# Query feature sums moved behind four half projections, and burst places of other double steps rewritten, in a gated mix of two linear-attention branches

## The chip, the cores and the metric

The kernel runs on one core of one Trainium2 chip. The metric is the device time of one execution in microseconds, as the median of the runs shown.

## The reference

One input x (2048 tokens, 640 features, 32 heads of 20) goes through two attention branches, A and B, and a gate mixes them:

```python
g = sigmoid((x * gate_w).sum(-1, keepdims=True))
a = A(x, wqkv, w_phi, wo)       # softmax features of q and k, linear attention over all tokens
b = B(x, wq, wk, wv, wo, beta)  # 4 segments of 512 tokens, local softmax plus a memory
return g * a + (1 - g) * b
```

Branch B is what the change touches. Its core, for each segment s:

```python
phi = lambda t: where(t > 0, t + 1, exp(t))
a_dot = softmax(qs @ ks.T * scale + causal_mask) @ vs
a_mem = (phi(qs) @ M) / (phi(qs) @ z + 1e-6)
o = sigmoid(beta) * a_mem + (1 - sigmoid(beta)) * a_dot
M, z = M + phi(ks).T @ vs, z + phi(ks).sum(tokens)
```

All inputs are bf16.

## The kernel before

Branch A comes first. It ends with a loop (L638 to L681) in which POOL adds the two halves of each token chunk (oA, L666) and SP turns the result (L674); meanwhile ACT evicts the first projections of branch B (L596), and SP turns them (L602). The query features of chunk 4, the first chunk of segment 1, have their exponential there too (L659), so that only their sum is left.

Branch B runs as 16 *double steps* (L966 to L996). A step is one group of four heads of one segment, a double step is two of them, a and b; four double steps make a segment. Each double step has five *bursts* of logits: PE multiplies keys by queries (L736, PSUM tile st_ps), and ACT takes the exponential of two tiles of 128x1024 (L740, into PT). POOL clears the triangles above the diagonal (L747). There are two st_ps tiles, so PE may run one tile ahead of ACT and then waits.

Between the bursts PE does other work, the *items*. A string of letters per double step (PLAN, L950) lists them in order, and a list of four shares per double step (SHARES, L955) says how far down the list PE gets after each of the first four bursts. After the fifth it does the rest. Every item has a weight, the estimated PE time in us; an item goes in after burst n as long as the weight done so far plus half its own is below share n of the whole (L992). The letters:

- h: half a projection of one chunk of 128 tokens for q, k or v of the next segment: five matmuls (L922), then an eviction of 128x320 by DVE (L928). With the second half of a q or k chunk, SP turns the chunk (L602).
- f and o: half an output row block, five or ten matmuls (L866), and its eviction by DVE (L875 or L877). A second half of f also stores the row (L879, on SP).
- A and D, B and C: the products of PT and values (L790), memory products (L798, L803) and the epilogue on DVE and POOL (L815 to L837), of step a of this double step (A, D) and of step b of the last one (B, C). Products go to one PSUM tile, nda.
- k and q, weight 0: the exponential of a chunk's features (L894, ACT).
- x and y, weight 0: the sum of a chunk's features for k and q, two DVE instructions (L897 takes the minimum with 1, L898 adds the positive part).
- z, weight 0: the transpose of the query features into the place of the consumed input (L907, on SP). It pairs with an earlier y.
- t, weight 0: the transpose of a finished chunk of branch B (L841, SP). u, weight 0: the four transposes of the last segment (L960, SP), which the closing part reads (L1046).

The matmuls of h, f and o write to one pool of two PSUM banks (tag ps1, L852). The third half in a row needs the bank of the first, and so the eviction of it.

The order on PE, ACT, DVE, POOL and SP is the order of the program (manual schedule): an instruction that waits holds all behind it on its engine. In double step 0 the halves h are the two halves of chunk 5 of k and the two of q, and the first y is the sum for chunk 4 of q.

Of the kernel before, what the change touches and what calls it, by code (L numbers as in the profile page):

```python
# [15 lines left out]
def kernel(  # L16
# [670 lines left out]
    with ExitStack() as bctx:  # L687
# [247 lines left out]
        def half_items(s, order):  # L935
# [11 lines left out]

        PLAN = ("qyhhhhozkxooAD", "qhhBhyChkzoxAooD", "qhhBhyChkzoxAooD",  # L950
                "ooBqoyoCokzoxADo", "hkhBhhChhqyhADztt", "khhBhxhqChfhyzAD",
                "khhBhxhqChfyzADt", "khhBhxhqChfyhzAD", "khhxtBhhqChyhADzt",
                "hhBhhqChfyhzAD", "hhBhhqCfhyzAthD", "hhBhhqhCftyhzAtD",
                "fBfCffADt", "fBftCfftAD", "fBftCffADf", "fuBfCfAfDf")
        SHARES = [[0.2, 0.42, 0.55, 0.77], [0.19, 0.4, 0.6, 0.85], [0.21, 0.4, 0.6, 0.8], [0.19, 0.4, 0.6, 0.81], [0.19, 0.41, 0.58, 0.8], [0.19, 0.41, 0.63, 0.86], [0.2, 0.4, 0.6, 0.83], [0.2, 0.4, 0.6, 0.83], [0.2, 0.4, 0.6, 0.8], [0.23, 0.4, 0.6, 0.82], [0.2, 0.4, 0.6, 0.82], [0.21, 0.4, 0.6, 0.82], [0.2, 0.4, 0.59, 0.8], [0.2, 0.39, 0.6, 0.8], [0.19, 0.4, 0.59, 0.8], [0.2, 0.4, 0.6, 0.85]]  # L955

        oT4 = oTA[:, 0:4]

# [7 lines left out]
        for dstep in range(NSEG * G // 2):  # L966
# [4 lines left out]
            items = []  # L971
            for w in PLAN[dstep]:
                if w in "hfo":
# [16 lines left out]
            for n, burst in enumerate(bursts(a, b)):  # L990
                burst()
                while items and (n == 4 or done + items[0][0] / 2 < SHARES[dstep][n] * whole):  # L992
                    w, fn = items.pop(0)
# [149 lines left out]
```

## Time and profile before

| what | us |
|---|---|
| median of three runs | 320.29 |
| the three runs | 320.96, 318.81, 320.29 |
| the profiled execution | 319.04 |
| its span on the core | 317.3 |
| PE busy / ACT busy / DVE busy / POOL busy | 303.7 / 252.8 / 225.4 / 209.2 |
| branch B's double steps, first exponential to the end of the last | 127.97 to 306.53 |

The span is the time from the first to the last recorded instruction of the profiled execution. Times of the trace count from the span's start. Busy times of PE overlap in a pipeline, so a busy PE need not be at its peak; a wait is what shows it held. The granted PE clock is 1.00 in every double step.

### The profile page before, as it was taken

What the parts mean: (1) busy time and instruction counts of PE and PEld (TensorE: products, weight loads), DVE (VectorE), ACT (ScalarE), POOL (GpSimd) and SP (SyncE); (2) the same over time, 40 slices, a digit from 0 to 9 for tenths busy, and PEclk for the clock granted to TensorE, in tenths of its full rate; (3) what the DMA queues carried; (4) which work ended last, traced back from release to release, by engine and by line L of the source; (5) the groups of instructions that cost most, each with busy time, mean ns of one, the idle gap of its engine ahead of it and who ended that gap; (6) DMA issues with size and microseconds to landing.
All of it is one profiled execution on the core that took longest, in us unless ns stands there. A gap on an engine that the chain in (4) does not pass through costs nothing.

```text
span 317.3 us, 9775 instructions
## 1 busy us (share of the span) xinstructions
PE 303.7 (96%) x4024; PEld 209.2 (66%) x4024; DVE 225.4 (71%) x505; ACT 252.8 (80%) x321; POOL 209.2 (66%) x308
## 2 busy tenths in 40 slices
PE   7999999999999999789999999999999999999995
PEld 7788877855578888356655566665656666656673
DVE  3477897998779997857668587778655864454463
ACT  5677888367846648799999899999989898898953
POOL 8588599103247989855656667778787777756550
PEclk9999999999999999999999999999999999999999
DMA  7949844439127989744331353473654443222132
GB/s 215 223 111 203 200 110 128 129 99 366 56 19 136 127 122 150 138 79 70 69 68 33 68 108 70 89 109 61 102 98 89 87 90 66 75 71 58 48 89 83
DMA packets 91814, 34.22 MB, mean 108 GB/s; under 512 B 79866, under 2 KB 91770, under 8 KB 91770
## 3 DMA queue, kind: packets, MB, share of 16 engines
q1 hardware_dynamic: 91194, 32.95, 49.3%
q10 hardware_dynamic: 576, 0.66, 0.8%
q8 instruction: 31, 0.51, 0.7%
q14 instruction: 13, 0.11, 0.1%
HBM read 6.42 MB, written 2.62 MB: 29 GB/s over the span
## 4 chain that ended last, share of the span: by engine, by line
PE 69%; ACT 21%; DVE 2%; issue 2%; DMA 2%; POOL 2%; SPq 1%; ACTq 0%; DVEq 0%; POOLq 0%
ACT PT L740 19%; PE st_ps L736 9%; PE proj L922 9%; PE proj L866 9%; PE pk L235 7%; PE pq L402 7%; PE pv L235 7%; PE nda L790 6%; PE proj L538 5%; PE num L460 3%; DMA x_nat<-in_A_x_dram 2%; PE kv_ps L375 2%; PE num L477 1%; DVE tt L508 1%; POOL oA L666 1%
## 5 line engine op out<-in xcount | busy, mean ns | idle before, releaser
L740 ACT ACTIVATE PT<-st_ps 128x1024 bf16<-128x1024 f32 x160 | 153.5, 1023 | 14.7 <-PE st_ps L736 12.7
L747 POOL TENSOR_SCALAR_AFFINE_SELECT PT<-PT 128x512 bf16<-128x512 bf16 (+1 forms) x130 | 87.0, 688 | 48.7 <-ACT PT L740 48.6
L790 PEld LDWEIGHTS <-PT 128*128 128x128 bf16 x1280 | 40.4, 96 | 9.6 <-issue 5.8
L790 PE MATMUL nda<-vB,PT 128*128 128x21 bf16 x1240 | 41.9, 173 | 0.1
L247 POOL TENSOR_TENSOR EkSn<-Ek,krec 128x1280 bf16<-128x1280 bf16 x15 | 35.1, 2360 | 8.8 <-DVE krec L246 8.1
L922 PEld LDWEIGHTS <-xTf 128*128 128x128 bf16 x300 | 26.4, 97 | 16.1 <-issue 7.7
L928 DVE CAST Z<-proj 128x320 bf16<-128x320 f32 x44 | 21.0, 488 | 21.3 <-PE proj L922 21.3
L235 PEld LDWEIGHTS <-xTf 128*128 128x128 bf16 x240 | 27.1, 113 | 5.8
L409 ACT ACTIVATE Eq<-pq 128x1024 bf16<-128x1024 f32 x20 | 19.4, 1021 | 12.3 <-PE pq L402 12.3
L243 DVE TENSOR_REDUCE ksum<-Ek 128x64 f32<-128x1280 bf16 x16 | 23.6, 1475 | 7.6 <-ACT Ek L239 7.4
L866 PE MATMUL proj<-WkA,oTA 128*128 128x320 bf16 x160 | 28.2, 300 | 0.0
L508 DVE TENSOR_TENSOR tt<-num,rr 128x640 f32<-128x640 f32 x32 | 25.0, 813 | 4.5 <-POOL rr L501 1.7
L239 ACT ACTIVATE Ek<-pk 128x640 bf16<-128x640 f32 x32 | 20.8, 702 | 9.2 <-PE pk L235 8.2
L666 POOL TENSOR_TENSOR oA<-tt 128x640 bf16<-128x640 f32 x16 | 24.7, 1550 | 5.2 <-DVE tt L508 5.0
L736 PE MATMUL st_ps<-Z 32*128 32x384 bf16 (+3 forms) x256 | 24.0, 299 | 3.9 <-ACT PT L740 3.3
L736 PE MATMUL st_ps<-Eq 32*128 32x512 bf16 (+3 forms) x256 | 24.7, 299 | 2.4 <-ACT PT L740 1.9
L402 PE MATMUL pq<-xTf,WqA 128*128 128x512 bf16 x100 | 22.2, 379 | 0.0
L830 POOL TENSOR_TENSOR oB<-td 128x320 bf16<-128x320 f32 x22 | 19.0, 863 | 4.1 <-DVE td L827 4.1
L866 PE MATMUL proj<-WvA,oT 128*128 128x320 bf16 x120 | 21.3, 300 | 0.0
L827 DVE TENSOR_TENSOR td<-nda,rec 128x640 f32<-128x640 f32 x23 | 19.0, 825 | 2.1
L922 PE MATMUL proj<-WqB,xTf 128*128 128x320 bf16 x110 | 17.8, 300 | 1.8 <-DVE Z L928 1.8
L538 PEld LDWEIGHTS <-xTf 128*128 128x128 bf16 x180 | 16.2, 97 | 4.6
(177 smaller groups left out, 548.6 us busy)
## 6 DMA issues: line engine op xcount, KB each, us to landing
Z<-EkSn SPq DMA_DIRECT2D x32, 160.0 KB, 2.8
out_dram<-orow SPq DMA_DIRECT2D x8, 160.0 KB, 1.8
out_dram<-oTA SPq DMA_DIRECT2D x6, 160.0 KB, 1.9
WvA<-in_A_wqkv_dram SPq DMA_DIRECT2D x2, 400.0 KB, 6.7
WvB<-in_B_wv_dram SPq DMA_DIRECT2D x1, 800.0 KB
WkB<-in_B_wk_dram SPq DMA_DIRECT2D x1, 800.0 KB, 6.7
WqB<-in_B_wq_dram SPq DMA_DIRECT2D x1, 800.0 KB, 8.4
WkA<-in_A_wo_dram SPq DMA_DIRECT2D x1, 800.0 KB, 10.1
```

The lines of the kernel that those rows point to most:

```text
L235: nc.tensor.matmul(ps[:, bk, 0:n], lhsT=key_tokens(c, sc), rhs=rhs, start=(c == 0), stop=(c == KC - 1))
L247: (nc.vector if sc == NCH - 1 else nc.gpsimd).tensor_tensor(out=EkSn[:, sc].rearrange("p s (h f) -> p (s h) f", f=DH), in0=Ek.rearrange("p ...
L402: nc.tensor.matmul(pq[:, half, :], lhsT=WqA[:, c, j * P:(j + 1) * P], rhs=xq[:, 2 * qb + half, c], start=(c == 0), stop=(c == KC - 1))
L508: nc.vector.tensor_tensor(out=tt[:, sgn].rearrange("p (b h) d -> p b h d", b=2), in0=ps, in1=csb, op=ALU.mult)
L538: nc.tensor.matmul(ps, lhsT=xq[:, sc // 4, cc, sc % 4 * P:(sc % 4 + 1) * P], rhs=W[:, cc, half * 320:(half + 1) * 320], start=(cc == 0), s ...
L666: nc.gpsimd.tensor_tensor(out=oA.rearrange("p (h d) -> p h d", d=DH), in0=tt[:, 0], in1=tt[:, 1], op=ALU.add)
L736: nc.tensor.matmul(ps[:, i - i0, o:o + L - c * P], lhsT=kT[32 * i:32 * i + 32, c * P:(c + 1) * P], rhs=qT[32 * i:32 * i + 32, c * P:L], st ...
L740: nc.scalar.activation(out=PT[:, i0:i0 + 2], in_=ps, func=ACT.Exp, scale=SCALE_B)
L747: nc.gpsimd.affine_select(out=v, in_=v, pattern=[[0, n_i], [1, P]], compare_op=ALU.is_ge, fill=0.0, base=0, channel_multiplier=-1)
L790: nc.tensor.matmul(nd[:, j, i], lhsT=block(st, c)[:, i, (j - c) * P:(j - c + 1) * P], rhs=vB[:, c, 4 * st.g + i, :], start=(c == 0), stop= ...
L866: nc.tensor.matmul(ps, lhsT=oT[:, k % KC], rhs=W[:, k % KC, hs], start=(k == 0), stop=(k == n - 1))
L922: nc.tensor.matmul(ps, lhsT=xq[:, sc // 4, k, sc % 4 * P:(sc % 4 + 1) * P], rhs=W[:, k, half * 320:(half + 1) * 320], start=(k == 0), stop ...
```

## The change

Only the letters and the shares differ:

```diff
-        PLAN = ("qyhhhhozkxooAD", "qhhBhyChkzoxAooD", "qhhBhyChkzoxAooD",
-                "ooBqoyoCokzoxADo", "hkhBhhChhqyhADztt", "khhBhxhqChfhyzAD",
+        PLAN = ("qhhhhyzokxooAD", "qhhBhyChkzoxAooD", "qhhBhyChkzoxAooD",
+                "ooBqoyoCokzoxADo", "hkhBhhChhqyhADztt", "khhBhxhqChfhyzAD",
...
-                "fBfCffADt", "fBftCfftAD", "fBftCffADf", "fuBfCfAfDf")
+                "fBfCfftAD", "fBftCfftAD", "fBtfCffADf", "fBfCufAffD")
```

In double step 0, y moves from ahead of the four h to behind them, and z follows it directly, ahead of the first o. In double step 12, t moves ahead of A; in 14, t moves ahead of the second f; in 15, u moves from ahead of B to behind C, and the last f from behind D to ahead of it.

The shares that differ, by double step:

```diff
- 2: 0.21, 0.4, 0.6, 0.8        4: 0.19, 0.41, 0.58, 0.8
+ 2: 0.19, 0.4, 0.6, 0.8        4: 0.19, 0.38, 0.58, 0.8
- 3: 0.19, 0.4, 0.6, 0.81       9: 0.23, 0.4, 0.6, 0.82
+ 3: 0.19, 0.4, 0.61, 0.79      9: 0.23, 0.39, 0.6, 0.82
- 10: 0.2, 0.4, 0.6, 0.82      11: 0.21, 0.4, 0.6, 0.82
+ 10: 0.2, 0.39, 0.6, 0.82     11: 0.21, 0.39, 0.6, 0.82
- 13: 0.2, 0.39, 0.6, 0.8      14: 0.19, 0.4, 0.59, 0.8
+ 13: 0.21, 0.39, 0.6, 0.8     14: 0.19, 0.37, 0.59, 0.81
- 15: 0.2, 0.4, 0.6, 0.85
+ 15: 0.2, 0.41, 0.6, 0.85
```

Worked out with the rule of L992, this is what changes place (bursts counted from 1):

| double step | before | after |
|---|---|---|
| 0 | y behind burst 1, ahead of all halves; z behind burst 4 | y and z behind burst 3, after the last two matmuls of the fourth half |
| 2 | five pieces of B (six PV matmuls) behind burst 1 | behind burst 2 |
| 3 | two pieces of A (six PV matmuls) behind burst 4 | behind burst 5 |
| 4 | one projection matmul behind burst 2 | behind burst 3 |
| 9, 10, 11 | | nothing moves |
| 12 | t behind D's epilogue | t ahead of A, behind the same burst 5 |
| 13 | one output matmul behind burst 2 | behind burst 1 |
| 14 | t behind burst 3; sixth matmul of (6,1) behind burst 2; one piece of A behind burst 5 | t behind burst 2, ahead of (6,1); that matmul behind burst 3; that piece behind burst 4 |
| 15 | u behind burst 1; one piece of C behind burst 3; two pieces of D behind burst 4; last half ends the double step | u behind burst 3, after C; that piece behind burst 2; one matmul of the last half behind burst 4, its rest ahead of D |

## The prediction

> **What bounds the kernel now.** I read the page first, then the busy time stretch by stretch, who waits for whom, and the timeline around the letters that move. The page's chain of waits, by engine:
>
> ```profile
> PE 69%; ACT 21%; DVE 2%; issue 2%; DMA 2%; POOL 2%; SPq 1%; ACTq 0%; DVEq 0%; POOLq 0%
> ```
>
> Almost all of the end is set by PE and ACT, and DVE has 2% of it. What an edit on DVE or SP is worth therefore hangs on the places where PE or ACT waits for it. The 16 double steps run from 127.97 us, the first exponential of L740, to about 306.5. I cut them at the first exponential of each; here are double steps 0, 1 and 12 to 15 (columns: stretch, width, busy time of each engine, clock, DMA share, GB/s):
>
> ```profile
> 127.97:140.08 12.11, 9.35 (x111) 5.22 (x111) 8.38 (x14) 9.98 (x12) 7.79 (x9) 1.00 0.69 132
> 140.08:150.98 10.90, 10.40 (x155) 6.48 (x155) 8.03 (x20) 10.59 (x13) 6.67 (x12) 1.00 0.32 52
> 263.05:274.43 11.38, 11.36 (x167) 7.19 (x166) 5.37 (x12) 9.69 (x10) 8.49 (x17) 1.00 0.26 59
> 274.43:284.72 10.29, 9.73 (x150) 6.01 (x149) 4.82 (x10) 9.59 (x10) 6.26 (x10) 1.00 0.26 65
> 284.72:295.63 10.91, 10.59 (x155) 6.52 (x155) 5.51 (x12) 9.67 (x10) 6.55 (x10) 1.00 0.27 72
> 295.63:306.53 10.90, 10.66 (x159) 7.30 (x159) 5.32 (x12) 9.62 (x11) 7.36 (x12) 1.00 0.27 69
> ```
>
> Double step 0 stands out: it has the least matmul work (9.35 us of PE) and takes longest (12.11). Neither PE nor ACT is full in it; in all the others one of them nearly is. Over all double steps PE waits for an eviction just once:
>
> ```profile
> PE st_ps L736 <- ACT PT L740: 5.2, 20, 0.5
> PE proj L922 <- DVE Z L928: 1.8, 1, 1.8
> ```
>
> The timeline shows that one wait in double step 0 (start, length, instruction, and in brackets the idle time before it):
>
> ```profile
> 128.12 3.12 POOL L666 TENSOR_TENSOR oA<-tt 128x640 bf16<-128x640 f32 x2
> ...
> 128.37 1.48 DVE L897 TENSOR_SCALAR Eq<-Eq 128x640 bf16<-128x640 bf16 x1
> ...
> 129.88 2.04 DVE L898 SCALAR_TENSOR_TENSOR Eq<-Z,Eq 128x640 bf16<-128x640 bf16 x1
> ...
> 131.84 0.88 DVE L928 CAST Z<-proj 128x320 bf16<-128x320 f32 x2
> 132.37 1.25 PE L922 MATMUL proj<-WqB,xTf 128*128 128x320 bf16 x8 [1.77 <-DVE Z L928]
> ...
> 133.99 3.77 ACT L740 ACTIVATE PT<-st_ps 128x1024 bf16<-128x1024 f32 x4 [1.84 <-PE st_ps L736]
> ```
>
> The letter y puts L897 and L898, the query feature sum, at the head of DVE's queue. The two evictions of the key half projections (L928, two in one row) stand behind them, the third half projection needs one of the two banks that they free, PE waits 1.77 us, and behind PE the exponentials of the third burst start 1.84 us late. The pair is slow only here: 1.48 + 2.04 = 3.52 us, while POOL's two L666 run beside it. All 19 later pairs take 1.14 to 1.64 us in sum (the first 0.34 + 0.83).
>
> **The change, part by part.** It adds and removes no operation; it reorders.
>
> *y behind four half projections.* Under the share rule y now stands behind the third burst and the last two matmuls of the second query half. DVE then does the casts of all four halves before L897 and L898. Redone from rows: the first key half ends at 129.29 (last start 128.99 + 0.30), and DVE, free at 128.45, casts it in 0.49 to 129.84. The second ends at 130.60 and is cast by 131.15. The first query half needs only the first bank and runs from 130.43; the second may start at 131.2 (0.1 us late), three of its matmuls follow at 0.136 us, and the third burst starts at 131.71. From its first matmul to its exponential it is 0.43 us (133.55 to 133.98), so the exponential starts at 132.14, where ACT is free at 132.05. Gain 133.98 − 132.14 = 1.84 us; 1.94 is the most, since consecutive exponentials overlap by 0.10.
>
> *What is late next.* The second query half ends near 132.97 and is cast by 133.5. Then L897, L898: at 1.21 us (the pair at 137.05, with gaps) they end at 134.75, just when the next output half's matmuls do; its cast, queued behind the pair, ends at 135.3, and the half that needs its bank starts 0.08 us late, which hides behind exponentials and the key exponential (L894, 0.76). That cover is about 0.1 us: beyond it, each microsecond of the pair costs one. At the slowest later pair (1.64) 0.4 us are lost. I take 0, as the median pair is 1.15 to 1.2. Casts of L928 beside L666 are not in the trace. The 60 it has take 0.474 to 0.494 us, those beside POOL's selects too; if one grew as L897 did (+1.16), the first query half would start at 131.05 and about 0.6 us would be lost. I take 0, by L508, which also reads PSUM, ran beside L666 and spans 0.760 to 0.826 over 32.
>
> The Trainium skill (SBUF — State Buffer, Who interferes with whom) says that VectorE and GpSimd share one port pair as an exclusive lock, and the second to come blocks for the whole of the other's instruction. The trace agrees in double step 0, where L898 ends 0.7 us after the second L666; beside selects most pairs keep their 1.15 us. By the rule each of the two could come second and stand behind one select, a rival below.
>
> *z.* It issues one transpose (L907) on SP's queue. Nothing of SP lies between its old and new place, so its order stays: the two turns L602, then L907. SP is busy with L674 until 132.7; L907 starts near 135.4 (136.22 now), lands 3.2 us later, and the next writer of its source (L898 of step 1) comes near 142.8. Cost nothing; 4 us of cover.
>
> *Rewritten letters and shares.* By the rule, double steps 9 to 11 keep every item in its place, and t in 12 has no SP instruction between its old and new place; t in 14 goes ahead of one row store on SP, with its reader some 12 us away: zero each. The rest move a few matmuls across a burst, which counts only where a wait of PE for ACT is filled or widened. From the waits before each burst: step 2, six PV matmuls later, second burst's exponential 0.14 earlier; step 3, six later (0.156), last burst earlier by 0.16; step 4, one matmul (0.137) put behind the wait at 177.37, 0.14 lost; step 13, one put into the wait at 276.42, 0.1 gained; step 14, one behind the wait at 289.04 and one PV piece ahead of the last burst, 0.2 lost; step 15, lighter third and fourth stretches, 0.17 gained. Sum −0.23, ends −0.9 and +0.9 (every one a gain, every one a loss).
>
> *u behind C.* Four transposes (L960, 5.31 us of SP) move behind the row store of (9,1), whose eviction ends at 299.88, so they start near 300.35, 2.5 us later than now, at 1.25 us each:
>
> ```profile
> 297.86 5.31 SPq L960 DMA_TRANSPOSE oTA<-oB  x4
> 303.26 0.52 SPq L879 DMA_DIRECT2D out_dram<-oTA  x1
> ```
>
> They land 2.4 us after issue: 302.8, 304.0, 305.3, 306.5. Their readers (L1046) run at 305.88, 308.09, 309.27 and 310.78: 3 us of cover at least. Stores queued behind them (rows 7 and 11) go out by 306.5 and 308, before the last ones at 312.96. The moved f and D keep PE's sum; the step's epilogue ends near 307.85 on DVE, before its reader at 308.9. Zero.
>
> **Sum.** −1.84 − 0.23 = −2.07 us. The profiled execution took 319.04 (span 317.3 and 1.74 around it): 316.97 after. The median of the three runs is 320.29, 1.25 above the profiled one; the same difference gives 318.2.
>
> **Rivals.**
> - *The wait moves along (ends slower).* If the pair stays at 3.52 us at its new place, DVE is busy to 137.1, the output half's cast to 137.6, the fourth half ends at 138.2 and the last burst starts near 138.3 against 137.82 now: 0.5 lost, 320.6. It turns at a pair of about 3.1 us. For it: POOL selects (L747) run there. Against: no L666 does (the last ends at 131.23), and 19 pairs stay under 1.64. Chance 0.06.
> - *Half-blocked pair.* Two waits of one select (median 0.64) make 2.4 us, 1.2 lost, 319.4; the trace's pairs never reach it. Chance 0.04; 318.8 for the milder 1.64 pair or slowed casts, 0.12.
> - *u comes late.* If it also waits for C's epilogue (L830, 303.10 to 303.96), the first lands at 306.4 to 308.1 (by 2.4, and by the 4.1 that L907 took at the longest), 0.5 to 2.2 late: 318.7 to 320.4. Against: today L830 writes while these transposes are in flight and waits for none of them. Chance 0.06.
> - *The letters win more.* PE's idle time in the seven rewritten steps is 0.75, 0.54, 0.38, 0.02, 0.56, 0.32, 0.24, in sum 2.8; half of it gone gives 320.29 − 1.84 − 1.4 = 317.05. Against: steps 4 and 14 go the other way. Chance 0.12.
>
> **How the numbers follow.** Forecast 0.60. A measurement of this kernel can tell about 1% (3.2 us) from no change. The three runs lie −1.5 to +0.7 about their median. Low: 318.2 less 0.7 for the letters and 1.0 for scatter, 316.5; high: the slower cases, 320.5. Faster by over 1% (under 317.1): half of the last rival, a tenth of the forecast, some scatter of the rest, 0.15. Slower by over 1% (over 323.5) needs two slow cases together, 0.04. Within: 0.81.
>
> **What would show it.** Right: PE's wait for L928 gone from the waits, double step 0 near 10.3 us, L897 + L898 near 1.2 us at about 133.5, all later steps within 0.3 us of now, L960 from about 298.3 (shifted) with no wait of PE for it. Wrong: a pair over 2 us, a new wait of PE for L877, a tail stretched at L1046, or steps 12 to 15 off by more than 0.5.

## The result and the profile after

| | before | changed |
|---|---|---|
| median, us | 319.9 (6 runs, 318.81 to 320.96) | 317.31 (6 runs, 316.97 to 317.53) |
| ratio, 95% interval | | 0.992 (0.9897 to 0.9944) |
| profiled execution, us | 319.04 | 317.34 |
| its span | 317.3 | 315.6 |
| first exponential of branch B | 127.97 | 128.32 |
| from there to the end of the span | 189.33 | 187.28 |
| double step 0 | 12.11 | 10.24 |

The change makes the kernel faster by 0.6 to 1.0%. The profiled execution of the changed kernel came to branch B 0.35 us later, with no changed instruction ahead of that place; so branch B is best compared by its own length, from its first exponential to the end of the span, which is 2.05 us less.

The page's chain of waits of the changed kernel, by engine:

```profile
PE 74%; ACT 21%; DVE 1%; DMA 1%; issue 1%; SPq 0%; ACTq 0%; DVEq 0%
```

DVE's share went from 2% to 1%. Who PE waits for, from 125 us to the end (total, times, longest):

```profile
PE st_ps L736 <- ACT PT L740: 3.6, 15, 0.3
PE st_ps L736 <- ACT vB L596: 0.2, 1, 0.2
```

The wait for L928 is gone, and nothing took its place. The waits for ACT fell too, from 5.2 us in 20 to 3.6 in 15. The timeline around y in double step 0:

```profile
128.47 3.05 POOL L666 TENSOR_TENSOR oA<-tt 128x640 bf16<-128x640 f32 x2
...
129.74 0.49 DVE L928 CAST Z<-proj 128x320 bf16<-128x320 f32 x1 [0.92 <-ACT PT L740]
...
130.55 5.68 ACT L740 ACTIVATE PT<-st_ps 128x1024 bf16<-128x1024 f32 x6 [0.29 <-PE st_ps L736]
...
130.78 1.31 PE L922 MATMUL proj<-WqB,xTf 128*128 128x320 bf16 x8
...
133.76 0.32 DVE L897 TENSOR_SCALAR Eq<-Eq 128x640 bf16<-128x640 bf16 x1
...
134.11 0.82 DVE L898 SCALAR_TENSOR_TENSOR Eq<-Z,Eq 128x640 bf16<-128x640 bf16 x1
...
135.12 0.49 DVE L877 CAST oTA<-proj 128x320 bf16<-128x320 f32 x1 [0.18 <-PE proj L866]
```

The first cast starts at once (beside L666, and at its usual 0.49 us), the query half follows the key half with no wait, and ACT runs six exponentials back to back where it had stood idle for 1.84 us. The pair L897, L898 takes 1.14 us instead of 3.52, and the cast behind it (L877) finds DVE idle. The double steps of the changed kernel, cut and laid out as in the prediction's table:

```profile
128.32:138.56 10.24, 9.57 (x111) 5.23 (x111) 6.55 (x14) 9.95 (x13) 7.83 (x9) 1.00 1.00 156
138.56:149.45 10.89, 10.40 (x155) 6.48 (x155) 8.01 (x20) 10.58 (x14) 6.65 (x12) 1.00 0.39 55
...
272.82:283.23 10.41, 10.14 (x152) 6.09 (x150) 4.81 (x11) 9.70 (x11) 6.38 (x11) 1.00 0.26 65
283.23:293.97 10.74, 10.48 (x155) 6.39 (x154) 5.86 (x12) 9.57 (x10) 6.41 (x10) 1.00 0.28 72
293.97:304.92 10.95, 10.63 (x159) 7.14 (x159) 5.19 (x12) 9.64 (x11) 7.31 (x12) 1.00 0.23 55
```

ACT is now busy in nearly all of double step 0 (9.95 of 10.24), which is 1.87 us shorter. Double step 1, untouched, has its old width to 0.01, and steps 5 to 12 have theirs to 0.02. Steps 2, 3 and 4 moved by −0.13, +0.08 and −0.01, steps 13, 14 and 15 by +0.11, −0.16 and +0.05: little in sum.

### The profile page after: what moved, and what is told of

It is laid out like the page before. It is cut to its first block, busy times and chain, and to the rows that moved or that the text cites. A ratio compares the mean times of both kernels' runs of the same rounds, so it can differ in the third digit from the quotient of the medians.

```text
span 315.6 us, 9776 instructions
## 1 busy us (share of the span) xinstructions
PE 305.0 (97%) x4024; PEld 210.1 (67%) x4024; DVE 223.9 (71%) x505; ACT 252.8 (80%) x321; POOL 209.1 (66%) x308
## 4 chain that ended last, share of the span: by engine, by line
PE 74%; ACT 21%; DVE 1%; DMA 1%; issue 1%; SPq 0%; ACTq 0%; DVEq 0%
ACT PT L740 18%; PE st_ps L736 10%; PE proj L922 9%; PE proj L866 9%; PE pk L235 7%; PE pq L402 7%; PE proj L538 7%; PE pv L235 7%; PE nda L790 6%; PE num L460 4%; PE kv_ps L375 2%; DMA wnat_k<-in_A_wqkv_dram 1%; PE num L477 1%; PE nda L798 1%; PE v_ps L538 1%
## 5 line engine op out<-in xcount | busy, mean ns | idle before, releaser
L928 DVE CAST Z<-proj 128x320 bf16<-128x320 f32 x44 | 21.1, 489 | 23.4 <-PE proj L922 22.4
L666 POOL TENSOR_TENSOR oA<-tt 128x640 bf16<-128x640 f32 x16 | 24.6, 1546 | 5.2 <-DVE tt L508 5.0
L736 PE MATMUL st_ps<-Z 32*128 32x512 bf16 (+3 forms) x256 | 24.7, 299 | 3.2 <-ACT PT L740 2.3
L866 PEld LDWEIGHTS <-oTA 128*128 128x128 bf16 x160 | 13.6, 97 | 8.0 <-issue 4.0
```

The lines of the kernel that those rows point to most:

```text
L666: nc.gpsimd.tensor_tensor(out=oA.rearrange("p (h d) -> p h d", d=DH), in0=tt[:, 0], in1=tt[:, 1], op=ALU.add)
L736: nc.tensor.matmul(ps[:, i - i0, o:o + L - c * P], lhsT=kT[32 * i:32 * i + 32, c * P:(c + 1) * P], rhs=qT[32 * i:32 * i + 32, c * P:L], st ...
L866: nc.tensor.matmul(ps, lhsT=oT[:, k % KC], rhs=W[:, k % KC, hs], start=(k == 0), stop=(k == n - 1))
```

## The experiments

All lengths of branch B below run from the first exponential to the end of the span, in the profiled execution: 189.33 us before, 187.28 after. The expectations call this end the last eviction; that ends some 2.7 us earlier in every trace (at 314.58 of 317.3 us before), so the differences are the same to 0.03. Double steps that a kernel leaves untouched, and that do not follow a changed one, repeat to about 0.02 us from trace to trace; the one exception was step 7 of the kernel with only the rest of the change, 0.13 shorter.

### The letter y alone

```diff
- "qyhhhhozkxooAD"
+ "qhhhhyzokxooAD"     (double step 0 only; all else as before)
```

> The kernel before with only double step 0 changed (y behind the four halves, z right behind it). Theory 'y held the bank': double step 0, from its first exponential to that of double step 1, shrinks from 12.11 to about 10.24 us as in the changed kernel, PE's wait for L928 is gone, and the time is 1.8 to 1.9 us below the kernel before; that is nearly all of the change. Rival 'the letters': the step's gain is given back later or is only part of the 2.6 us between the medians, and this kernel gains less than 1.5 us.

Measured: 317.49 us against 319.48 for the kernel before, ratio 0.993 (0.9913 to 0.9946). Double step 0 takes 10.24, branch B 187.46, and the list of PE's waits has no L928. This letter, with z behind it, gives 1.87 of the 2.05 us; the rival that the other letters matter falls.

### The rest alone

```diff
- "qhhhhyzokxooAD"
+ "qyhhhhozkxooAD"     (all other double steps as changed)
```

> The changed kernel with double step 0 as before: only the rewritten letters and shares of double steps 2 to 15. Theory 'y held the bank': double step 0 is 12.1 us again with a wait of PE for L928 of 1.8 us, and the rest gives 0 to 0.3 us (forecast 0.23; the two traces differ by 0.18 after double step 0). Rival 'the letters': 0.7 us or more faster than before.

Measured: 319.27 us, ratio 0.9992 (0.9976 to 1.0007): no difference that the times can tell. Branch B takes 189.08, 0.25 less than before, of which 0.13 is the step 7 named above and does not come from the change, so that 0.12 is left. Double step 0 takes 12.13 again. PE's wait is back:

```profile
PE st_ps L736 <- ACT PT L740: 4.1, 16, 0.5
PE proj L922 <- DVE Z L928: 1.8, 1, 1.8
```

### y first, but POOL quiet

```diff
+ if ch >= NCH - 2: nc.gpsimd.memset(oA, 0.0)
+ else:
      nc.gpsimd.tensor_tensor(out=oA..., in0=tt[:, 0], in1=tt[:, 1], op=ALU.add)
```

> The kernel before, y still first in double step 0, but the last two sums of branch A on POOL (L666, chunks 14 and 15) are replaced by filling their tile with zeros, so that POOL reads no SBUF while y runs; the branch A rows of these two chunks are left out of the result. Theory 'the length of the pair, made by POOL': L897 + L898 take 1.15 to 1.3 us at the head of the queue, the first cast ends near 130.1, PE's wait for L928 is below 0.2 us and double step 0 takes 10.2 to 10.4 us with y in its old place. Rival 'the place in the queue alone': a wait of PE above 0.5 us stays, and the step stays above 10.9 us.

Measured: 317.54 us, ratio 0.9936 (0.9917 to 0.9955); branch B 187.78, double step 0 10.54. The pair and PE's wait for a cast in this kernel, whose lines are three further down (minimum, median and longest in ns; then total, times, longest):

```profile
L900 DVE TENSOR_SCALAR Eq<-Eq x1: 1116/1116/1116, 128.3 to 128.3; 128x640 bf16<-128x640 bf16 x1
...
L901 DVE SCALAR_TENSOR_TENSOR Eq<-Z,Eq x1: 826/826/826, 129.4 to 129.4; 128x640 bf16<-128x640 bf16 x1
```

```profile
PE proj L925 <- DVE Z L931: 0.2, 1, 0.2
```

With y still at the head of the queue 1.57 of the 1.87 us come back: the pair is 1.58 us shorter and PE's wait 1.56 (1.77 to 0.21). So it was the length of the pair, made by POOL's L666, that cost the time, and the place in the queue only where it met that length. The forecast of the pair was missed: 1.12 + 0.83 = 1.94 us in sum, not 1.15 to 1.3. The filling with zeros reads no SBUF, and still the minimum beside it was three times as long as at a quiet place (0.32). Step 0 therefore lands at 10.54, between the two expected figures and nearer to the first.

### y behind two halves

```diff
- "qyhhhhozkxooAD"
+ "qhhyhhozkxooAD"
```

> The kernel before with y behind the two key halves only, ahead of the two query halves; z in its old place. If only the two casts in front of the waiting half matter: PE's wait for L928 is below 0.4 us, the pair takes 1.2 to 1.6 us (the last L666 ends just after it starts), and the gain is 1.5 to 1.85 us. If the pair must also stay clear of POOL's L666 and of the query casts: the pair takes over 2 us, the output half waits for its bank, and the gain is under 1.2 us.

Measured: 317.36 us, ratio 0.9924 (0.9907 to 0.9942); double step 0 10.35, branch B 187.60. PE waits for no eviction by DVE. The pair takes 0.32 + 1.15 us, since L666 ends at its start:

```profile
131.04 0.32 DVE L897 TENSOR_SCALAR Eq<-Eq 128x640 bf16<-128x640 bf16 x1
131.39 1.15 DVE L898 SCALAR_TENSOR_TENSOR Eq<-Z,Eq 128x640 bf16<-128x640 bf16 x1
132.46 1.03 DVE L928 CAST Z<-proj 128x320 bf16<-128x320 f32 x2
```

The gain is 1.73 us, with z in its old place, so z is not needed for it. It is enough that the two casts which free the banks stand ahead of the pair, at least for a pair as short as it is there: this run does not keep the pair long, so it does not part the place from the length. The place behind four halves is worth another 0.11 to 0.14 us in the trace and nothing that the times can tell.

### A longer pair at the new place

```diff
- nc.vector.tensor_scalar_min(out=ek, in0=ek, scalar1=1.0)
+ for _ in range(5 if (part, sc) == ("q", 4) else 1):     (3 in the second kernel)
+     nc.vector.tensor_scalar_min(out=ek, in0=ek, scalar1=1.0)
```

> The changed kernel with the minimum of the first y (L897, 0.32 us at the new place) done five times instead of once; doing it again changes no value. The pair grows by about 1.3 to 1.4 us. Forecast's step 'that cover is about 0.1 us, beyond it each microsecond costs one': double step 0 takes 11.3 to 11.6 us instead of 10.24, the output half waits for its bank (a wait of PE for L877 of about 1 us), and the end moves by as much. Rival 'DVE has room there': double step 0 below 10.6 us.

> The changed kernel with the minimum of the first y done three times. With five, the pair grew from 1.17 to 3.85 us, PE waited 2.30 us for L877, double step 0 grew by 2.74 and double step 1, at a granted clock of 0.50 for some 3 us, by another 0.74. With three the pair should grow by 0.7 to 1.5 us. Forecast's step 'each microsecond costs one': double step 0 grows by the pair's growth less 0.1. Theory 'the clock falls when PE waits over 2 us': the wait is below 1.8 us, double step 1 stays at 10.9 us and the clock at 1.00. If any wait of PE here lowers the clock: double step 1 is 0.3 us longer or more.

| minima | pair, us | PE's wait for L877 | double step 0 | double step 1 | branch B |
|---|---|---|---|---|---|
| 1 | 1.17 with gaps | none | 10.24 | 10.89 | 187.28 |
| 3 | 2.68 | 1.14 | 12.50 | 10.88 | 189.55 |
| 5 | 3.85 | 2.30 | 12.98 | 11.63 | 190.78 |

Each of the two kernels was run once (319.70 us with three minima, 320.56 with five). The rival that DVE has room there falls. Most of what was expected in figures missed. With five minima the pair grew by 2.7 us, not by 1.3 to 1.4: its third and fourth minimum, beside POOL's selects, took 0.80 and 0.64 us instead of 0.32. And with three, double step 0 grew by 2.26 us instead of the pair's growth less 0.1 (1.4). On the clock, one theory had it stay at 1.00 and the other had step 1 grow; it fell, but in step 0, and step 1 kept its width. PE's wait in the kernel with five minima, then in the one with three:

```profile
137.78 0.70 PE L866 MATMUL proj<-WkA,oTA 128*128 128x320 bf16 x4 [2.30 <-DVE oTA L877]
```

```profile
136.96 1.07 PE L866 MATMUL proj<-WkA,oTA 128*128 128x320 bf16 x4 [1.14 <-DVE oTA L877]
```

The wait itself does go one for one: it is the pair's growth less 0.37 to 0.38 us in both kernels (1.51 and 1.14, 2.68 and 2.30). Branch B grew by more than the wait, by 1.13 us more with three minima (2.27) and 1.20 more with five (3.50). The granted clock shows where the rest may come from. Stretches of the kernel with five minima, then of the one with three (the columns are those of the double steps above; the clock is the third figure from the end):

```profile
137.70:138.80 1.10, 1.02 (x13) 0.46 (x13) 1.06 (x4) 0.00 (x0) 0.00 (x0) 1.00 0.18 37
138.80:140.30 1.50, 1.50 (x49) 1.34 (x46) 0.82 (x3) 1.45 (x2) 0.00 (x0) 0.82 0.85 159
140.30:141.30 1.00, 1.00 (x6) 0.20 (x4) 0.77 (x3) 0.78 (x2) 0.44 (x1) 0.50 0.00 0
141.30:142.30 1.00, 1.00 (x6) 0.57 (x5) 0.31 (x2) 1.00 (x2) 1.00 (x3) 0.50 0.00 0
142.30:143.80 1.50, 1.50 (x16) 0.76 (x14) 0.49 (x1) 1.27 (x2) 1.00 (x3) 0.71 0.00 0
143.80:144.70 0.90, 0.90 (x33) 0.69 (x32) 0.49 (x1) 0.48 (x1) 0.00 (x0) 1.00 0.00 0
```

```profile
136.96:137.20 0.24, 0.24 (x2) 0.19 (x2) 0.22 (x1) 0.00 (x0) 0.04 (x1) 0.92 0.38 73
137.20:140.60 3.40, 3.40 (x59) 1.88 (x57) 1.91 (x4) 1.94 (x2) 0.00 (x0) 0.50 0.43 82
140.60:144.00 3.40, 3.31 (x48) 1.98 (x46) 2.17 (x6) 3.12 (x4) 2.48 (x5) 1.00 0.00 0
```

Behind the wait the clock falls to 0.50 for about 3.4 us: 0.2 us after its end with three minima, all in step 0, and 2.0 us after it with five, reaching into step 1. How the loss comes about shows best with three: the matmuls of the fifth burst start 9.59 us after the first exponential, earlier than the 9.86 before the change, and the step still ends 0.39 us later than before, with the low clock in between. The theory that only a wait over 2 us goes with this does not hold: here it was 1.14 us, in the one execution that there is.

### The rewritten double steps, one by one

Each kernel is the one with y alone (187.46) plus one double step of the change. Each was run once, and their times (317.17 to 317.56 us) cannot be told apart, so the lengths of branch B have to do. Double step 3 has one more edit than the list of the change shows: its letter x, the key feature sum, goes ahead of an output half, behind the same burst.

```diff
- "ooBqoyoCokzoxADo"
+ "ooBqoyoCokzxoADo"     (double step 3)
```

> The kernel before with double steps 0 and 2 of the change only. Forecast's term: 0.14 faster than 187.46, 187.32. Rival, from the trace after, where step 3 behind it is longer by 0.1: PE gives it back in step 3, 187.42 to 187.50.

> The kernel before with double step 0 and double step 3 of the change only. Measured from the first exponential to the last eviction, the kernel with double step 0 alone takes 187.46 us. Forecast's term: 0.16 faster, 187.30. Rival 'the cut': the last burst of step 3 comes earlier but PE, which is full from there into step 4, gives it back, 187.44 to 187.50.

> The kernel before with double steps 0 and 13 of the change only. Forecast's term: 0.1 faster than 187.46, 187.36, by a matmul that fills PE's wait in the first burst. Rival, from the trace after, where step 13 is 0.11 longer: the second burst's exponential is late by as much, 187.45 or more.

> The kernel before with double steps 0 and 14 of the change only. Forecast's term: 0.2 slower than 187.46, 187.66, by a matmul behind PE's wait at the third burst and a piece of A ahead of the last. Rival, from the trace after, where step 14 is 0.16 shorter: 187.30 to 187.45.

> The kernel before with double steps 0 and 15 of the change only, u behind C among it. From the first exponential to the last eviction the kernel with double step 0 alone takes 187.46 us. Forecast's term: 0.17 faster, 187.29, and L960's transposes near 298 with no wait of PE for them. Rival 'u comes late': a wait of PE at L1046 and 188 or more. Rival 'order of the end only': 187.40 to 187.50.

| double step | forecast, us | branch B, us | measured against 187.46, us |
|---|---|---|---|
| 2 | −0.14 | 187.42 | −0.04 |
| 3 | −0.16 | 187.40 | −0.06 |
| 13 | −0.10 | 187.32 | −0.14 |
| 14 | +0.20 | 187.53 | +0.07 |
| 15 | −0.17 | 187.33 | −0.13 |
| 4, with 12, by subtraction from 187.28 | +0.14 | not run alone | +0.12 |

All signs are as forecast, but hardly one is larger than the stray 0.13 us of step 7 above, so a single term is not shown by its one trace. By the bounds set beforehand, step 2 goes to the rival (PE gives it back), 13 and 15 go to the forecast, and 3 and 14 lie between the two. The term of step 3 holds its shares and the letter x together. In step 2 the gain is there (11.09 against 11.24) and step 3 behind it gives 0.10 back; in step 13 it is the other way, the step itself grows by 0.11 and step 14 shrinks by 0.25. A step's own width therefore does not tell what an edit in it is worth. In the kernel with y and step 15 the transposes of u start 4.7 us into the step instead of 2.2, and PE waits for none of them (SP's queue; in this kernel the line of u is L956):

```profile
292.01 6.81 SPq L879 DMA_DIRECT2D out_dram<-oTA  x2
298.91 5.08 SPq L956 DMA_TRANSPOSE oTA<-oB  x4
304.08 0.52 SPq L879 DMA_DIRECT2D out_dram<-orow  x1
```

### A version picked from these

```diff
  double steps 0, 2, 3, 13, 15 as changed; 4, 12 and 14 as before
- [0.2, 0.42, 0.55, 0.77]      (shares of double step 0)
+ [0.16, 0.37, 0.55, 0.77]
```

> A version meant to beat both: double steps 0, 2, 3, 13 and 15 of the change, 4 and 14 as before (their terms were losses), and in double step 0 two matmuls fewer ahead of the second burst and two fewer ahead of the third (shares 0.16, 0.37), which should take away the 0.29 us that ACT idles there. If the terms add up: 0.2 to 0.3 us less in double step 0 (9.95 to 10.05), and 0.1 to 0.2 in 4 and 14, so 186.8 to 187.0 from first exponential to last eviction against 187.28 for the changed kernel. Rival 'PE gives it back': 187.2 to 187.4.

Measured: 317.21 us, ratio 0.9915 (0.9894 to 0.9936); branch B 187.08, 0.20 below the changed kernel. That is the sum of the steps left out (0.12 + 0.07), and lies between the two expectations (186.8 to 187.0, and 187.2 to 187.4). The new shares of step 0 gave nothing: it stays at 10.24, because ACT's idle time went from the second burst to the third:

```profile
128.00 3.90 ACT L740 ACTIVATE PT<-st_ps 128x1024 bf16<-128x1024 f32 x4
132.15 3.77 ACT L740 ACTIVATE PT<-st_ps 128x1024 bf16<-128x1024 f32 x4 [0.24 <-PE st_ps L736]
```

Its branch B is the shortest of all; by the times (317.21 and 317.31, not measured side by side) it cannot be told from the changed kernel.

## Why the prediction was right, point by point

- *What bounds the kernel, and y.* Right, in the mechanism too: the step "Gain 133.98 − 132.14 = 1.84 us" measured 1.87 in double step 0, y alone gives it, and shortening the pair in its old place gives most of it back. (PE's list before also has 0.2 us for an eviction by ACT, L596, at the first burst; it is there after the change too.)
- *What is late next.* The pair at its new place took 1.17 us with gaps (forecast 1.21), and L877 follows with no wait. The cast beside L666, which the trace before did not show, took 0.49: the value taken was right. The size of the cover was off: 0.37 us measured in both longer kernels, not about 0.1. "Beyond it each microsecond costs one" held for PE's wait and was too small for the time, which grew by 1.1 to 1.2 us more than the wait; in both traces the clock falls to 0.50 there.
- *The rival "The wait moves along".* Its price left out the clock. It was put at 0.5 us over the time before for a pair of 3.52 and at a turning point of 3.1. A pair of 2.68 us already made branch B 0.22 longer than before, one of 3.85 made it 1.45 longer. So where the clock falls, the turning point is below 2.7; with PE's wait alone (1.14) branch B would be about 188.4, an estimate, and a pair of 2.68 still a gain.
- *z and u.* Right: L907 starts at 135.94 (forecast 135.4, with branch B 0.35 later), L960 at 298.68 (298.3), and PE waits for neither.
- *Rewritten letters and shares.* The sum came out, −0.18 against −0.23, and that is partly luck: steps 2 and 3 were put 0.20 us too high as gains, step 14 0.13 too high as a loss, and the errors cancel. The letter x of step 3 was not seen and got no term; in the kernels that have it PE waits for no cast behind it.
- *The sum.* −2.07 us was worked out, −2.05 measured in branch B. The median fell by 2.59, probably because the median before is taken over executions of two kinds, as the last section argues; the forecast's 1.25 us between the profiled execution and the median before was carried over to the changed kernel (318.2), and there the median and the profiled execution are 0.03 apart.

## What to carry to other kernels

Work of weight zero on a queue is not free. Ahead of an eviction that another engine needs, it costs as much as its length exceeds the room there (1.77 us of wait for a pair of 3.52), and that length must be read from the place where it will run: 3.52 us beside POOL, 1.14 a few microseconds later. Where a double-buffered loop has PE wait for a cast, look first at what stands ahead of that cast on its engine. Price a wait of PE with what follows it, not with its own length alone: here 1.1 to 1.2 us came on top.

## What the runs showed of the hardware that was not expected

A wait of PE of 1.14 us, and one of 2.30, were each followed by 3.4 us at a granted clock of 0.50, in one execution each. The Trainium skill (TensorE: Matmul & The Clock Gate, Why this matters for your kernels) puts the limit at idle gaps of about 3 us; here less was enough. The Trainium skill (the same page, Part 1: The HAM clock gate) says that the activity is judged in free-running windows of 3.4 us; the length of the low clock fits that.

The wait of 1.77 us in double step 0 seems to do the same in part of the executions. Two kernels have it, the one before (29 executions whose clock was recorded) and the one with only the rest of the change (12). By their mean clock:

| kernels | mean clock | executions | mean time, us |
|---|---|---|---|
| with the wait | 0.993 to 0.995 | 17 of 41 | 320.29 |
| with the wait | 0.998 to 1.000 | 24 of 41 | 319.23 |
| ten kernels in which PE waits 0.2 us or not at all for an eviction | 0.998 to 1.000 | 31 of 31 | |

Half clock for 3.4 us in a span of 317 makes a mean of 0.995, which fits, and so does the price: the 17 executions are 1.05 us longer, the two with a longer pair 1.1 to 1.2 beyond their wait. Means just below 1.000 can come from the end: in the profiled execution of the kernel with only the rest (0.999) the clock falls to 0.50 for the last 0.8 us, after PE's last matmul. The two profiled executions with the wait had clocks of 1.000 and 0.999, so no trace shows where the clock fell in the 17; that it is behind this wait is argued from the two kernels with a longer pair, and from the kernel with y alone, which differs in y and z only, has no such wait and kept its clock in 6 of 6. It would explain the narrow spread of the changed kernel (0.56 us, against 2.15 before) and the half microsecond by which the medians differ more than the traces: the executions of the kernel before with a clock of 0.998 or more (17 of its 29, by chance the same number) have a mean of 319.33 us, the changed kernel has 317.28, and the difference is 2.05 us, as in the traces.

How much POOL lengthens the pair hangs on which of the two starts first, a point that the prediction left open. Of the 19 later L898 in the trace before, the 12 that start ahead of every select running beside them take 0.82 to 0.83 us, and the three that start 0.11 to 0.34 us behind the start of a select take 1.13 to 1.21.
